# Value loads of five transfers a pair in place of seven, in a chunked-attention and Fourier-mixing kernel

## The chip, the cores and the metric

The kernel runs on one core of one Trainium2 chip. A core has five engines that each run a queue of their own in order: TensorE (PE in the profile, with its weight loads as PEld), VectorE (DVE), ScalarE (ACT), GpSimd (POOL) and SyncE (SP). Transfers between device memory and on-chip memory are issued by SP, ACT and POOL and carried by 16 DMA engines. The metric is the device time of one execution in microseconds (us), the median over the runs of a kernel.

## What is computed

The first half is attention in chunks with memory keys. There are 4 batches, 8 heads, 768 positions and a head size of 64. Each chunk of 32 queries sees 8 memory keys, up to 16 keys to its left, its own 32 and up to 8 to its right. The second half mixes the result with a two-dimensional Fourier transform (its real part), adds it, normalises each row and runs a two-layer network with 2048 hidden units. The part that the change touches is this:

```python
for c in range(nc):
    c_start = c * chunk
    c_end = c_start + chunk
    l_start = max(0, c_start - left_ctx)
    r_end = min(S, c_end + right_ctx)
    k_full = np.concatenate([mem_k, k[:, :, l_start:r_end]], axis=2)
    v_full = np.concatenate([mem_v, v[:, :, l_start:r_end]], axis=2)
    scores = scale * np.matmul(q[:, :, c_start:c_end], k_full.transpose(0, 1, 3, 2))
    a = np.exp(scores - np.max(scores, axis=-1, keepdims=True))
    a = a / (np.sum(a, axis=-1, keepdims=True) + 1e-09)
    out[:, :, c_start:c_end] = np.matmul(a, v_full)
```

## The kernel before, in words

**Tiles.** The work goes by pairs of heads, 16 in all (n = 0 to 15, four for each batch); hh is the head within a pair. Two chunks share a tile of 64 queries, so a head has NT = 12 tiles. The keys of a tile lie on partitions: 0 to 7 the memory keys, 8 to 23 the left context, 24 to 87 the tile's own 64 keys, 88 to 95 the right context, which makes KEYS = 96. What one of the two chunks may not see is masked in the exponential by a bias per partition, `mbias`, one column for each half of the queries.

**A pair's steps.** `e_load_qk` (L383) loads queries and keys from POOL's queue. `e_turn_q` and `e_turn_k` transpose them on PE (L415, into PSUM tiles trq and trk). `e_qT` (L433) copies the queries out on ACT; `e_kT` (L458; L453 for the last batch) copies the keys out with their overlap of left and right context, on DVE for n = 0 to 2, on ACT for n = 3 to 11 and on DVE again for the last batch. `e_scores` (L471) or `a_scores` (L494) multiplies, `e_exp` (L481) or `a_exp` (L506) takes the exponential, `e_values` (L523) multiplies the exponentials with the values in 48 small matmuls a pair (tiles xa and xo), and `e_norm` (L533, L534) divides by the sum, which column 64 of the value tile supplies through a column of ones. Each of the four value tiles `va` holds one pair in fp32, so a pair's values can be loaded once the pair that used its tile before it (n - 4) has been multiplied.

**The value loads.** `e_load_v` issues seven transfers a pair: the own keys of tile 0 for both heads (L399), and then for each head the run of 80 keys (left context and own keys) for tiles 1 to 11 (L392), the right context of 8 keys for tiles 0 to 10 (L392), and the 8 memory values for all tiles (L405). Every descriptor moves one row of 64 fp32 values, 256 bytes. All go through SP's queue, except that in the first batch the second head's long run is issued by ACT. `e_edges` zeroes what tile 0 lacks on its left and the last tile on its right, and `e_edge_ones` takes the ones from the sum column there; both run on POOL, for the first buffer partly on DVE.

**The order.** The kernel plans its order by costs, but the order on each engine is then fixed by lists at the end of the kernel, so the emission order is the same in both kernels. The scheduling layer gives each transfer that SP or ACT issues one of eight landing semaphores, in turn and in the order of the program. A transfer waits, besides for its buffer, until the one that had its semaphore before it, eight transfers of these two queues earlier, has landed. A queue is in order, so whatever stands behind such a transfer waits too. PE's queue also holds a fixed number of filler matmuls (L1040, L1048, tile dz), which do no work for the result.

**The rest.** After its pairs a batch is folded and multiplied with tables of sines (L729 and L768 for batch 0, L595 and later lines for the others), turned round and normalised, and then goes through the network (L908, L926, L975). The network's weights are loaded by POOL in eight transfers (L1269, L1274) during batch 1. For the batches after the first, rows travel out and back through device memory (L629, L633, L638).

Of the kernel before, what the change touches and what calls it, by code (L numbers as in the profile page):

```python
# [14 lines left out]
ALU = mybir.AluOpType  # L15

CHUNK = 32
LEFT = 16
RIGHT = 8
NMEM = 8  # L20
BIGM = 800.0
MEM0 = 0
OWN = MEM0 + NMEM + LEFT
KEYS = OWN + 2 * CHUNK + RIGHT


def rev_ap(src, last, count, outer=()):
# [5 lines left out]
def strided(src, off, dims):  # L33
    return bass.AP(tensor=src.tensor, offset=src.offset + off,
                   ap=[list(src.ap[0])] + [list(d) for d in dims])


class Plan:
# [14 lines left out]
    filling, fill, fine = None, None, None  # L53
# [155 lines left out]
def kernel(  # L209
# [11 lines left out]
    nc = tc.nc  # L221
    B, H, S, D = q.shape
    DM = out.shape[2]
    DFF = moe_w_ch1.shape[1]
    P = 128
# [3 lines left out]
    NT = S // 64  # L229
    RB = 8  # L230
    QP = S // RB
    KP = QP + 4
# [40 lines left out]
    NKT = 2  # L273
    KR, NKU = 16, 2
    kU = [spool.tile([P, KR + S + KR], BF16, name=f"kU{i}") for i in range(NKU)]
    kTb = [spool.tile([P, NT, P], BF16, name=f"kTb{i}") for i in range(NKT)]
# [36 lines left out]
    mbias = cpool.tile([P, 2], FP32)  # L313
# [24 lines left out]

    def e_masks():
        nc.gpsimd.memset(mbias, 0.0)  # L340
        nc.gpsimd.memset(mbias[64:96, 0:1], NEG)
        nc.gpsimd.affine_select(out=mbias[:, 1:2], in_=mbias[:, 1:2], compare_op=ALU.is_ge,
                                fill=NEG, base=-(OWN - LEFT + CHUNK), pattern=[[0, 1]],
                                channel_multiplier=1)
        nc.gpsimd.memset(mbias[MEM0:MEM0 + NMEM, 1:2], 0.0)
# [5 lines left out]
    def e_edges(i):  # L351
        v1, eng = va[i], nc.vector if i < 1 else nc.gpsimd
        eng.memset(v1[:, :, :, D:D + 1], 1.0)  # L353
        eng.memset(v1[0:32, :, 0, 0:D], 0.0)
        eng.memset(v1[64:96, :, NT - 1, 0:D], 0.0)

    def e_edge_ones(i):
        v1 = va[i]
        lo, hi = v1[0:32, :, 0, D:D + 1], v1[64:96, :, NT - 1, D:D + 1]
        nc.gpsimd.affine_select(out=lo, in_=lo, compare_op=ALU.is_ge, fill=0.0, base=-OWN,  # L360
                                pattern=[[0, 2], [0, 1]], channel_multiplier=1)
        nc.gpsimd.affine_select(out=hi, in_=hi, compare_op=ALU.is_ge, fill=0.0,
                                base=OWN + 63 - 64, pattern=[[0, 2], [0, 1]],
                                channel_multiplier=-1)
        nc.gpsimd.memset(v1[MEM0:MEM0 + NMEM, :, 0, D:D + 1], 1.0)

    def e_mkf():
# [18 lines left out]
    def e_load_v(n, half=None):  # L386
        b, pr = seq[n]
        v1 = va[n % NV]

        def run(p0, count, t0, nt, key, hh, by):  # L390
            vb = v[b, 2 * pr + hh]
            by.dma_start(v1[p0:p0 + count, hh, t0:t0 + nt, 0:D],  # L392
                              bass.AP(tensor=vb.tensor, offset=vb.offset + key * D,
                                      ap=[[D, count], [64 * D, nt], [1, D]]))

        if half == 1:
            run(OWN - LEFT, LEFT + 64, 1, NT - 1, 64 - LEFT, 1, nc.scalar)
            return
        nc.sync.dma_start(v1[OWN:OWN + 64, :, 0, 0:D],  # L399
                          v[b, 2 * pr:2 * pr + 2, 0:64].rearrange("h p d -> p h d"))  # L400
        for hh in range(2):
            if half is None or hh == 0:
                run(OWN - LEFT, LEFT + 64, 1, NT - 1, 64 - LEFT, hh, nc.sync)
            run(OWN + 64, RIGHT, 0, NT - 1, 64, hh, nc.sync)
            nc.sync.dma_start(v1[MEM0:MEM0 + NMEM, hh, :, 0:D],  # L405
                              mem_v[b, 2 * pr + hh].unsqueeze(1).to_broadcast([NMEM, NT, D]))

# [41 lines left out]

    def e_kT(n, eng=None):  # L450
        if n >= TURNED * HP:
            win = LEFT + 64 + RIGHT
            nc.vector.tensor_copy(  # L453
                strided(kTb[n % NKT], MEM0 + NMEM, [[P, NT], [1, win]]),
                strided(kU[n % NKU], KR - LEFT, [[64, NT], [1, win]]))
            return
        trk = tr_of.pop((n, 1))
        (eng or nc.scalar.copy)(  # L458
            strided(kTb[n % NKT], MEM0 + NMEM, [[P, NT], [RB, 11], [1, RB]]),
            strided(trk, 0, [[64 // RB, NT], [1, 11], [KP, RB]]))  # L460
        if n < 2 or n in JOINED:
            let_go(trk)

# [47 lines left out]
    def e_values(n, g):  # L511
        e1 = e1_of.pop((n, g))
        if g == 1:
            xa = bank("mlp" if n < HP else pick_of["v", n]["tag"], [P, 3, 2, 66], FP32, "xo")
        else:
            xa = aps.tile([P, 3, 2, 66], FP32, tag="xa", bufs=1, name="xa")
        xa_of[n, g] = xa
        for st in range(3):
            for hh in range(2):
                v1 = va[n % NV]  # L520
                for half in range(2):
                    t6 = 2 * st + half
                    nc.tensor.matmul(xa[64 * half:64 * half + 64, st, hh, 0:65],  # L523
                                     e1[0:KEYS, hh, t6, :], v1[0:KEYS, hh, 6 * g + t6, 0:65],
                                     start=True, stop=True)

    def e_norm(n, g):
# [1170 lines left out]
```

## Time and profile before

| What | Value |
|---|---|
| time, median of 3 runs | 272.72 us (272.63 to 278.22) |
| the profiled execution, its own time | 271.1 us |
| its span, first to last instruction | 269.4 us |
| PE busy, share of the span | 260.8 us, 97% |
| DVE, ACT and POOL busy | 202.7, 162.8 and 89.6 us |
| packets moved, bytes | 116118, 40.00 MB |
| of these under 512 bytes | 104560 |
| granted TensorE clock | 1.0 |

A busy share is an average over stages with different limits. The chain of waits follows the end of the program back, step by step, to what released each instruction. In a timeline row the numbers are the start and the length in us, then engine, line, operation and tiles, and in brackets how long the engine stood idle before it and what ended that. An engine name with a q behind it (SPq, ACTq) is that engine's queue issuing a transfer; the length then holds the time that the issue waited as well. In a row of a group the numbers behind the bar are busy us, mean ns of one instruction, and idle us before them. In a table by stretches each engine's busy us are followed by its number of instructions, and the last three numbers are the granted clock, the mean share of the DMA engines in use and GB/s.

### The profile page before, as it was taken

The page shows a single profiled execution, that of the slowest core. Times are in us where ns is not written, and L with a number is a line of the kernel's source. Part 1 is how long each engine was busy: PE and PEld are TensorE (multiplying, and loading weights), DVE is VectorE, ACT ScalarE, POOL GpSimd, SP SyncE. Part 2 cuts the span into 40 slices and gives each one's busy share as a digit, 9 for nine tenths or more (in the row PEclk, how much of TensorE's full clock was granted, in tenths as well). Part 3 has the DMA queues.
Part 4 walks back from the last instruction along what each step waited for, and adds up shares of the span by engine and source line. Part 5 has one row for each costly group of instructions (what it writes and reads, how often), then busy time and mean ns, then how long its engine had stood idle before and what let it go on. Part 6 is the DMA issues. An engine that isn't in the chain of part 4 may idle for free.

```text
span 269.4 us, 8363 instructions
## 1 busy us (share of the span) xinstructions
PE 260.8 (97%) x3469; PEld 215.8 (80%) x3469; DVE 202.7 (75%) x456; ACT 162.8 (60%) x318; POOL 89.6 (33%) x159
## 2 busy tenths in 40 slices
PE   6999899999999999999899999999999999999995
PEld 6556597888964778857798888888988988888884
DVE  6867488863379779999999989999887855354444
ACT  6757868899866279766742974726627171715150
POOL 7985463045120091564480550006006231000000
PEclk9999999999999999999999999999999999999999
DMA  6999999979998999989999974681913233334263
GB/s 102 206 180 191 211 195 200 213 126 195 197 241 169 130 218 175 126 222 206 197 218 161 159 169 88 165 130 19 238 20 82 61 77 80 89 61 108 56 166 92
DMA packets 116118, 40.00 MB, mean 148 GB/s; under 512 B 104560, under 2 KB 111472, under 8 KB 116080
## 3 DMA queue, kind: packets, MB, share of 16 engines
q1 hardware_dynamic: 90304, 22.64, 46.5%
q0 software_dynamic: 21472, 15.21, 34.8%
q10 hardware_dynamic: 4304, 1.62, 3.0%
q8 instruction: 27, 0.44, 0.7%
q14 instruction: 11, 0.09, 0.1%
HBM read 37.36 MB, written 13.37 MB: 188 GB/s over the span
## 4 chain that ended last, share of the span: by engine, by line
PE 73%; DVE 11%; DMA 8%; POOL 4%; issue 1%; SPq 1%; ACT 0%; POOLq 0%
PE ph L908 27%; PE pc L975 21%; PE pc L926 5%; PE ps L595 5%; DMA va<-in_v_dram 5%; DMA va<-in_mem_v_dram 3%; PE xa L523 3%; PE xo L523 3%; PE ps L729 2%; PE pm L768 2%; DVE st L843 1%; DVE xsb L534 1%; PE pm L789 1%; DVE xsb L817 1%; PE sc L494 1%
## 5 line engine op out<-in xcount | busy, mean ns | idle before, releaser
L908 PE MATMUL ph<-unT,w_sb 128*128 128x256 f16 x768 | 88.9, 273 | 0.2 <-DVE xsb L980 0.2
L917 ACT ACTIVATE hT<-ph 128x512 f16<-128x512 f32 x96 | 55.2, 600 | 51.6 <-PE pc L975 37.5
L908 PEld LDWEIGHTS <-w_sb 128*128 128x128 f16 x768 | 74.2, 98 | 9.7 <-issue 0.5
L975 PEld LDWEIGHTS <-hT 128*128 128x128 f16 x360 | 34.6, 98 | 4.5 <-DVE hT L963 0.2
L975 PE MATMUL pc<-w_sb,hT 128*128 128x256 f16 x288 | 36.6, 273 | 0.0
L980 DVE TENSOR_TENSOR xsb<-pc,xsb 128x256 f32<-128x256 f32 x64 | 26.1, 419 | 13.7 <-PE pc L975 12.8
L831 POOL TENSOR_TENSOR xsb<-mix,xr 128x512 f32<-128x512 f32 x9 | 12.3, 1384 | 42.3 <-ACT mix L825 24.4
L506 ACT ACTIVATE e<-sc,mbias 96x192 f32<-96x192 f32 (+1 forms) x48 | 19.0, 470 | 5.0 <-PE sc L494 5.0
L926 PE MATMUL pc<-w_sb,hT 128*128 128x512 f16 x96 | 21.7, 379 | 0.0
L481 ACT ACTIVATE e<-sc,mbias 96x384 f32<-96x384 f32 x32 | 17.0, 573 | 6.8 <-PE sc L471 6.8
L963 DVE TENSOR_TENSOR S<-hT 128x768 f16<-128x768 f16 (+1 forms) x18 | 7.6, 421 | 17.2 <-ACT hT L917 16.9
L857 ACT ACTIVATE un<-xsb,rs 128x512 f16<-128x512 f32 x18 | 14.4, 821 | 5.3 <-POOL rs L872 5.3
L975 PE MATMUL pc<-w_t,S 128*128 128x256 f16 x144 | 17.4, 273 | 0.0
L926 PEld LDWEIGHTS <-hT 128*128 128x128 f16 x96 | 9.1, 98 | 10.1
L843 DVE BATCH_NORM_STATS2 st<-xsb 128x6 f32<-128x512 f32 x24 | 16.3, 681 | 0.8 <-POOL xsb L831 0.6
L523 PE MATMUL xa<-va,e 96*64 96x65 f32 x384 | 14.9, 226 | 1.3 <-DMA va<-in_mem_v_dram 1.3
L523 PEld LDWEIGHTS xa<-va,e 96*64 96x64 f32 x384 | 12.6, 137 | 3.7 <-issue 2.9
L975 PEld LDWEIGHTS <-S 128*128 128x128 f16 x144 | 14.0, 98 | 1.6
L523 PE MATMUL xo<-va,e 96*64 96x65 f32 x384 | 14.1, 223 | 0.0
L1040 PE MATMUL idle<-dz 128*128 128x512 bf16 x46 | 12.9, 387 | 1.0 <-DVE va L353 1.0
L433 ACT COPY qT<-trq 128x768 bf16<-128x768 bf16 x12 | 9.6, 796 | 6.6 <-PE trq L415 6.4
L523 PEld LDWEIGHTS xo<-va,e 96*64 96x64 f32 x384 | 12.6, 138 | 0.4 <-ACT e L481 0.2
(192 smaller groups left out, 489.1 us busy)
## 6 DMA issues: line engine op xcount, KB each, us to landing
va<-in_v_dram SPq DMA_DIRECT2D x28, 220.0 KB
w_sb<-in_moe_w_ch_dram POOLq DMA_DIRECT2D x8, 512.0 KB, 9.0
out_dram<-xsb SPq DMA_DIRECT2D x12, 256.0 KB
qs<-in_q_dram POOLq DMA_DIRECT2D x12, 192.0 KB, 6.7
ks<-in_k_dram POOLq DMA_DIRECT2D x12, 192.0 KB, 6.6
x_rows<-xsb POOLq DMA_DIRECT2D x3, 768.0 KB, 5.1
xr<-x_back POOLq DMA_DIRECT2D x3, 768.0 KB, 5.7
out_rows<-xsb SPq DMA_DIRECT2D x9, 256.0 KB
```

Of the source, the lines that this page charges most:

```text
L481: nc.scalar.activation(e1[0:KEYS, :, :, ts(half, 32)], sc[0:KEYS, :, 0:6, ts(half, 32)], AFT.Exp, bias=mbias[0:KEYS, half:half + 1], scale ...
L506: nc.scalar.activation(to, src, AFT.Exp, bias=mbias[0:KEYS, half:half + 1], scale=1.0 / math.sqrt(D))
L523: nc.tensor.matmul(xa[64 * half:64 * half + 64, st, hh, 0:65], e1[0:KEYS, hh, t6, :], v1[0:KEYS, hh, 6 * g + t6, 0:65], start=True, stop=True)
L595: nc.tensor.matmul(out_[:, sp, :], part[:, ab, sp * 3 + st, c0:c1], tab[:, sp, st, :], start=(st == 0 and i == 0), stop=(st == 2 and i == 1))
L843: nc.vector.bn_stats(st6, xs[b][:, kt, :])
L857: nc.scalar.activation(un, xs[b][:, kt, :], AFT.Identity, bias=rs[:, 1:2], scale=rs[:, 0:1])
L908: nc.tensor.matmul(ph[:, k, :], w1_sb[:, dt, ts(HH * k + i, P)], unT_of[b, j][:, dt, :], start=(dt == 0), stop=(dt == NDT - 1))
L917: nc.scalar.activation(hT_of[b, j][:, :, i, :], ph, AFT.Relu, bias=0.0, scale=1.0 if (b, j) in FAST else -1.0)
L926: nc.tensor.matmul(pc_of[b, j, r], hT_of[b, j][:, k, i, ts(r, P)], w2_sb[:, HH * k + i, :], start=(i + k == 0), stop=(i + k == HH))
L975: nc.tensor.matmul(pc_of[key], a[:, i, :], w[:, i, :], start=(i == 0 and new), stop=(i == HH - 1), skip_group_check=not new)
L980: nc.vector.tensor_tensor(u, pc, u, ALU.add)
L1040: nc.tensor.matmul(fill_of[0], dz, strided(dz, 0, [[0, 4], [1, P]]), start=True, stop=True)
```

## The change

The value run of a tile gets 8 keys more than any chunk sees: AFTER = 16 keys follow the tile's own 64, and KEYS becomes 104. With that, one run of 96 keys for tiles 1 to 11 takes the place of the run of 80 and of the right context's own transfer, and tile 0's transfer takes 80 keys. A pair's loads are then five: tile 0 for both heads, and a run and the memory values for each head. The 8 extra keys are masked for both halves by `mbias`. The run of the last tile would read past the head's end, where the next head's rows lie; the values matmul of the last tile therefore takes only its first LAST = 88 partitions, and the very last head of the input, behind which nothing lies, has its last tile in a transfer of its own. The zeroing on the right and its part in the ones go away. The copies of the keys take 96 columns a tile in place of 88, and the exponentials 104 partitions in place of 96.

```diff
-KEYS = OWN + 2 * CHUNK + RIGHT
+AFTER = 2 * RIGHT
+LAST = OWN + 2 * CHUNK
+KEYS = LAST + AFTER
...
         nc.gpsimd.memset(mbias, 0.0)
-        nc.gpsimd.memset(mbias[64:96, 0:1], NEG)
+        nc.gpsimd.memset(mbias[64:P, 0:1], NEG)
+        nc.gpsimd.memset(mbias[96:P, 1:2], NEG)
...
         eng.memset(v1[0:32, :, 0, 0:D], 0.0)
-        eng.memset(v1[64:96, :, NT - 1, 0:D], 0.0)
...
-        lo, hi = v1[0:32, :, 0, D:D + 1], v1[64:96, :, NT - 1, D:D + 1]
+        lo = v1[0:32, :, 0, D:D + 1]
...
-        nc.gpsimd.affine_select(out=hi, in_=hi, compare_op=ALU.is_ge, fill=0.0,
-                                base=OWN + 63 - 64, pattern=[[0, 2], [0, 1]],
-                                channel_multiplier=-1)
...
+        def rows(hh, by):
+            whole = (b, 2 * pr + hh) != (B - 1, H - 1)
+            run(OWN - LEFT, KEYS - OWN + LEFT, 1, NT - 2 + whole, 64 - LEFT, hh, by)
+            if not whole:
+                run(OWN - LEFT, LEFT + 64, NT - 1, 1, S - 64 - LEFT, hh, by)
+
         if half == 1:
-            run(OWN - LEFT, LEFT + 64, 1, NT - 1, 64 - LEFT, 1, nc.scalar)
+            rows(1, nc.scalar)
             return
-        nc.sync.dma_start(v1[OWN:OWN + 64, :, 0, 0:D],
-                          v[b, 2 * pr:2 * pr + 2, 0:64].rearrange("h p d -> p h d"))
+        nc.sync.dma_start(v1[OWN:KEYS, :, 0, 0:D],
+                          v[b, 2 * pr:2 * pr + 2, 0:64 + AFTER].rearrange("h p d -> p h d"))
         for hh in range(2):
             if half is None or hh == 0:
-                run(OWN - LEFT, LEFT + 64, 1, NT - 1, 64 - LEFT, hh, nc.sync)
-            run(OWN + 64, RIGHT, 0, NT - 1, 64, hh, nc.sync)
+                rows(hh, nc.sync)
             nc.sync.dma_start(v1[MEM0:MEM0 + NMEM, hh, :, 0:D],
                               mem_v[b, 2 * pr + hh].unsqueeze(1).to_broadcast([NMEM, NT, D]))
...
-            win = LEFT + 64 + RIGHT
+            win = LEFT + 64 + AFTER
...
-            strided(kTb[n % NKT], MEM0 + NMEM, [[P, NT], [RB, 11], [1, RB]]),
-            strided(trk, 0, [[64 // RB, NT], [1, 11], [KP, RB]]))
+            strided(kTb[n % NKT], MEM0 + NMEM, [[P, NT], [RB, 12], [1, RB]]),
+            strided(trk, 0, [[64 // RB, NT], [1, 12], [KP, RB]]))
...
                     t6 = 2 * st + half
+                    rows = LAST if 6 * g + t6 == NT - 1 else KEYS
                     nc.tensor.matmul(xa[64 * half:64 * half + 64, st, hh, 0:65],
-                                     e1[0:KEYS, hh, t6, :], v1[0:KEYS, hh, 6 * g + t6, 0:65],
+                                     e1[0:rows, hh, t6, :], v1[0:rows, hh, 6 * g + t6, 0:65],
                                      start=True, stop=True)
```

The order of the instructions on every engine is otherwise unchanged. The landing semaphores are handed out over five transfers a pair, so other transfers share one: in the built program ACT's transfer for n = 3 waits for the landing of n = 1's first run in place of n = 1's tile 0.

## The prediction, made before the changed kernel was run

> **What bounds the kernel now.** I read the page's first part, then the chain of waits in order of time, then a table of the stretches that this chain divides.
>
> ```profile
> span 269.4 us, 8363 instructions
> PE 260.8 (97%) x3469; PEld 215.8 (80%) x3469; DVE 202.7 (75%) x456; ACT 162.8 (60%) x318; POOL 89.6 (33%) x159
> ```
> ```profile
> 8.62 7.09 DMA va<-in_v_dram
> 15.73 0.59 SPq L399
> ...
> 17.01 5.83 DMA va<-in_v_dram
> 22.85 0.27 SPq L392
> 23.16 9.32 DMA va<-in_mem_v_dram
> 32.62 0.80 PE xa L523 x20
> ```
> ```profile
> 32.60:41.10 8.50, 8.48 (x134) 7.97 (x135) 5.75 (x13) 6.16 (x13) 5.50 (x14) 1.00 1.15 197
> 45.80:98.60 52.80, 52.80 (x845) 40.25 (x847) 36.11 (x75) 38.28 (x68) 14.62 (x24) 1.00 1.05 183
> 98.60:130.00 31.40, 30.68 (x450) 24.06 (x450) 30.87 (x65) 23.97 (x57) 15.39 (x21) 1.00 1.28 191
> 180.00:266.00 86.00, 86.00 (x812) 76.96 (x810) 55.05 (x130) 38.51 (x75) 13.64 (x20) 1.00 0.37 85
> ```
>
> The chain runs through the value loads up to 32.6 us, and through PE after that. It looks as if 24 us of loading were to be won, but a chain shows only the last arrival. PE was busy all that time too, with fillers, transposes and attention whose number and order are fixed. What the loads cost is PE's idle time in front of the matmul that waited:
>
> ```profile
> 30.95 0.34 PE L523 MATMUL xa<-va,e 96*64 96x65 f32 x4
> ...
> 32.62 0.80 PE L523 MATMUL xa<-va,e 96*64 96x65 f32 x20 [1.33 <-DMA va<-in_mem_v_dram]
> ```
>
> In the view of waits this is the only wait of PE for a value load, 1.33 us, for the last memory values of n = 3. From 32.6 us to the end PE is dense (the table's first number behind the stretch is PE's busy time), so what is gained here stays gained, and nothing else that the loads do can shorten the time. In the stretch from 98.6 to 130 us DVE is dense as well.
>
> **Part 1, the loads start earlier: minus 1.33 us.** The last value transfers of n = 3 were late because their issues were held in SP's queue, and then because they met the weights:
>
> ```profile
> 15.73 0.59 SPq L399 DMA_DIRECT2D va<-in_v_dram  x1
> ...
> 23.16 0.31 SPq L405 DMA_DIRECT2D va<-in_mem_v_dram  x1
> ```
> ```profile
> 22.94 1.12 POOL L1269 DMA_DIRECT2D w_sb<-in_moe_w_ch_dram  x2
> ```
>
> The first transfer of n = 2 went out at 15.73 us, when n = 1's run, eight transfers ahead, had landed (the chain: 8.62 + 7.09 = 15.71). The last of n = 3 went out at 23.16, just behind two weight loads of 512 KB each, and took 9.32 us where the right context of n = 2, issued at 17.01 and as small, took 5.83. With five transfers a pair, eight places reach back more than a pair and a half. Followed through the changed order, tile 0 and run of n = 2 wait only for n = 0's memory values and go out near 10 us; tile 0 and run of n = 3 wait for n = 1's memory values, issued right behind its run, near 17 us; the last memory values of n = 3 wait for an ACT transfer of n = 1 and for n = 2's tile 0, and I put them at 19 us. With those 5.83 us they land near 25 us, and even with 9.32 us near 28.5, ahead of the 30.95 at which PE asks. So the whole stall goes. What is late next at that place is PE itself. The bounds of this part are 0 and -1.33 us.
>
> **Part 2, a new wait in ACT's queue: plus 0.2 us.** The changed hand-out of semaphores moves the wait that stood in SP's queue at 15.73 into ACT's. ACT's transfer for n = 3 now waits for n = 1's run, and behind it stands the copy of n = 1's queries:
>
> ```profile
> 13.35 0.32 ACTq L392 DMA_DIRECT2D va<-in_v_dram  x1
> 13.76 0.57 ACT L481 ACTIVATE e<-sc,mbias 96x384 f32<-96x384 f32 x1
> 14.22 0.79 ACT L433 COPY qT<-trq 128x768 bf16<-128x768 bf16 x1
> 16.21 1.04 ACT L481 ACTIVATE e<-sc,mbias 96x384 f32<-96x384 f32 x2 [1.20 <-PE sc L471]
> ```
> ```profile
> 13.54 0.51 PE L415 MATMUL trq<-ident_b,qs 96*64 96x96 bf16 x16
> ...
> 17.27 0.54 PE L415 MATMUL trk<-turn_b,ks 100*64 100x100 bf16 x16
> ...
> 18.28 0.35 PE L471 MATMUL sc<-qT,kTb 64*128 64x64 bf16 x12
> ```
>
> The copy would start at L, the landing of n = 1's run, and not at 14.22. It frees the PSUM tile that PE's trk at 17.27 writes, and the exponentials behind it (1.04 us) free the scores' tile for PE at 18.28. A release took 14.22 - (13.54 + 0.51) = 0.17 us. So PE is held when L + 0.79 + 0.17 passes 17.27, or L + 0.79 + 1.04 + 0.17 passes 18.28: both from L = 16.3 us on, and from there each us of L costs PE one, because PE's fillers don't shrink. L was 15.71. For the changed L:
>
> ```profile
> DMA packets 3153, 0.93 MB, mean 199 GB/s; under 512 B 2977, under 2 KB 3152, under 8 KB 3152
> ...
> q10 hardware_dynamic: 1618, 0.41, 57.4%
> q1 hardware_dynamic: 1339, 0.33, 50.9%
> ```
> ```profile
> 8.72 1.33 POOL L362 TENSOR_SCALAR_AFFINE_SELECT va<-va 32x2 f32<-32x2 f32 x1
> ...
> 11.14 0.65 POOL L383 DMA_DIRECT2D qs<-in_q_dram  x1
> ```
>
> The first fence is the DMA view from 11 to 15.7 us: SP (q1) and ACT (q10) moved 2957 packets in 4.7 us, 629 a us. Tile 0 and run of n = 1 grow from 128 + 880 to 160 + 1056 packets, 208 more, or 0.33 us, and twice that when ACT's longer runs take turns with them. POOL loses a memset and a select for each buffer, among them the select of 1.33 us, so its query load at 11.14 starts up to about 1.8 us earlier and gets ahead of the run: 192 KB at 199 GB/s, up to 0.97 us. Against that, SP's issue for n = 1 no longer waits for a memset that ends at 8.1, some 0.4 us. L lies between 15.3 (none of the delays) and 15.71 + 0.66 + 0.97 = 17.3; the middle is 16.3, just where the cost begins. The cost is 0 to 1.0 us, and I take 0.2, as half of the cases lie below the threshold. If the cover is gone altogether, this part eats most of part 1.
>
> The Trainium skill speaks against the change here: its page "DMA: Bandwidth & Descriptors", section "Bandwidth", says that small descriptors pay a fixed overhead for each packet, so fewer transfers of more packets cost more. The page of the profile agrees: 90304 packets on SP's queue (q1) took 46.5% of 16 engines' span, 22 ns each, so 208 more cost 0.29 us of all engines for a pair, less than the 0.33 us above, which goes by the same count.
>
> ```profile
> q1 hardware_dynamic: 90304, 22.64, 46.5%
> ```
>
> The skill's same page, section "Why a DMA increments its semaphore by 16 and not by 1", says that a transfer of SP or ACT over 8 partitions uses only the lowest 8 of the 16 engines; no row here shows which engines. By that rule the fullest engines would go from 8 + 110 + 46 = 164 to 10 + 132 + 24 = 166 packets a pair, an estimate of 1% and not 9%, and rival C below would fall away; the sum would stay, since it prices the run, which uses all 16.
>
> **Part 3, wider copies and more rows: plus 0.2 us.**
>
> ```profile
> L415 PE MATMUL trk<-turn_b,ks 100*64 100x100 bf16 x192 | 6.4, 209 | 0.0
> L415 PE MATMUL trq<-ident_b,qs 96*64 96x96 bf16 x192 | 6.2, 207 | 1.1 <-DVE ident_b L1015 1.1
> ...
> L458 DVE COPY kTb<-trk 128x1056 bf16<-128x1056 bf16 x3 | 3.8, 1253 | 1.7 <-PE trk L415 1.7
> ```
> ```profile
> L453 DVE COPY kTb<-kU x4: 402/426/428, 117.4 to 157.3; 128x1056 bf16<-128x1056 bf16 x4
> ```
> ```profile
> L523 PE MATMUL xa<-va,e 96*64 96x65 f32 x384 | 14.9, 226 | 1.3 <-DMA va<-in_mem_v_dram 1.3
> ...
> L523 PE MATMUL xo<-va,e 96*64 96x65 f32 x384 | 14.1, 223 | 0.0
> ```
>
> The copies grow from 1056 to 1152 columns, by 9%: 0.11 us for each of the three early ones on DVE, about the same for the nine on ACT, 0.04 for the four of the last batch. The early ones stand ahead of PE's scores, with fillers as cover; without that cover they would cost 0.34 us, and I take 0.1. ACT's nine lie beside dense PE: nothing, or 1.0 us uncovered. The four lie in DVE's dense stretch, 0.15 us, of which I take 0.1. The value matmuls go from 96 to 104 rows. The nearest rows are transposes with 100 and with 96 rows, 209 and 207 ns with 100 and 96 columns, so 4 more rows show nothing of their own: 0. As an upper bound in proportion to the rows, the value matmuls' busy time of 14.9 + 14.1 = 29.0 us would grow by 8.3%, 2.4 us. The removed memsets and selects on POOL, and one memset more there, touch only part 2.
>
> **The sum.** -1.33 + 0.2 + 0.2 = -0.9 us. The profiled execution took 271.1 us with a span of 269.4, and would take 270.2. The median of the runs shown, 272.72, lies 1.6 us above the profiled one, so on that scale I forecast 271.8 us.
>
> **The rivals.**
>
> A: the wait only moves. L becomes 17.3 us or later, PE stands at trk for 1.0 us or more, and with the 0.2 of part 3 the stall's 1.33 us are used up: 272.6 us. For it speaks that SP, ACT and POOL compete in those microseconds; against it that SP issues earlier.
>
> B, the other side: more rows cost PE time. It decides as soon as a value matmul takes over 3% longer, since 3% of 29.0 us is 0.9. In full proportion: 272.72 - 0.9 + 2.4 = 274.2 us. The transposes speak against it.
>
> C: volume. Each pair moves 2464 packets and not 2256. Before, the last weights went out at 64.80 us; 11.7 us later, the longest landing of a weight load, they were there, at 76.5; PE's matmuls that read this layer begin at 77.80:
>
> ```profile
> 64.80 1.59 POOL L1274 DMA_DIRECT2D w_sb<-in_moe_w_ch_dram  x2
> ```
> ```profile
> DMA to landing us min/median/max: 7.3/9.0/11.7
> ```
> ```profile
> 77.80 4.32 PE pc L926 x20
> ```
>
> If all the 9% fell on that landing, it would be 1.1 us later and just meet PE's 77.80. With twice that PE would lose 1 us: 272.8 us. Only the last quarter of these weights is so late and it is read last, which speaks against it, as do the earlier starts of the value loads.
>
> D: no effect. The last values of n = 3 meet the weights anyway and land when PE asks or later, with the stall as before: 272.9 us with part 3.
>
> **How the numbers follow.** The forecast has a chance of 0.58, A 0.18, B 0.08, C 0.06, D 0.06, and 0.04 is left for what I don't see. The likeliest case by itself reaches from full gain without costs, 272.72 - 1.33 = 271.4, to 272.4. The median of another set of runs can differ by some tenths; I take 270.8 as the low end, which also covers part of the 1.6 us between the two scales, and 273.4 as the high end, which takes in A, C, D and half of B. About 2% is what a measurement of this kernel can tell from no change, 5.5 us here. No case comes near it in either direction, so within 2% has 0.94, and slower, where unseen waits can add up on a dense PE, 0.04; faster 0.02.
>
> **What would show it.** Part 1: no idle time before L523's matmuls near 31 us, n = 3's last L405 issue before 21 us. Part 2: the ACTq row at 13.35 moves to the landing of n = 1's run, and L433's copy with it; an idle time of PE before trk near 17 us is its price. Part 3: L458 at about 1.37 us on DVE, L523 still at 222 ns. The prediction is wrong if PE's idle time grows anywhere after 33 us, if L523 gets longer, or if the stall at 32.6 us stays.

## The result, and the profile after

The changed kernel took 272.92 us (median of 22 executions, 271.31 to 276.08), the kernel before 271.88 us (22, 269.56 to 278.24). Over the executions that can be compared the ratio is 1.0095, with an interval of 1.007 to 1.012: about 2.6 us of 270 slower, and not 0.9 us faster. Medians are over all executions, while ratios leave out those that were disturbed, so the two need not agree. Of the 19 executions of the changed kernel in the ratio, ten have a mean granted clock of 0.999 or 1.0, with spans of 269.6 to 271.4 us, and nine have 0.988 or 0.994, with spans of 271.0 to 273.3 us.

The profiled execution, one of the nine, took 273.75 us, with a span of 272.0 us against 269.4. The page's first part, and then the chain of waits from 7.5 to 21 us (start, duration, what):

```profile
span 272.0 us, 8306 instructions
PE 263.5 (97%) x3469; PEld 217.7 (80%) x3469; DVE 202.9 (75%) x455; ACT 163.9 (60%) x318; POOL 87.5 (32%) x153
```
```profile
8.12 10.07 DMA va<-in_v_dram
...
18.22 0.32 ACTq L391
...
18.58 0.81 ACT qT L437
...
19.43 0.56 PE trk L419 x16
```

n = 1's run was issued 0.5 us earlier than before and took 10.07 us instead of 7.09, so L, its landing, is 18.20 and not 15.71 us. ACT's transfer for n = 3 goes out at 18.22 (before: 13.35), the query copy behind it at 18.58 (14.22), and trk starts at 19.43 instead of 17.27. PE's timeline gives the idle time, and the table of stretches what came behind it; the column that ends the engines' busy times is the granted clock:

```profile
19.43 0.56 PE L419 MATMUL trk<-turn_b,ks 100*64 100x100 bf16 x16 [1.99 <-ACT qT L437]
```
```profile
17.30:20.00 2.70, 0.71 (x18) 0.59 (x18) 0.00 (x0) 1.42 (x3) 1.48 (x2) 0.97 1.36 183
20.00:23.00 3.00, 3.00 (x39) 1.91 (x40) 2.08 (x4) 1.39 (x3) 0.00 (x0) 0.50 1.31 198
23.00:24.00 1.00, 1.00 (x15) 0.34 (x13) 0.69 (x2) 0.00 (x0) 0.00 (x0) 0.88 1.23 185
24.00:32.60 8.60, 8.33 (x189) 5.67 (x181) 5.83 (x12) 6.67 (x12) 4.11 (x7) 1.00 1.00 161
```

PE stood for 1.99 us, and then worked at half its clock for some 3.4 us: from 20 to 23 us it ran 39 matmuls. By the clock column, 0.03 of 2.7 us, 0.50 of 3 us and 0.12 of 1 us weren't granted, together 1.7 us that are lost while PE counts as busy. So in this execution the one wait cost 1.99 + 1.7 = 3.7 us, and the second part shows in no list of waits, only in the clock. The ten executions with a mean clock of 0.999 or more can have no such stretch, since it takes 0.006 off the mean (1.7 of 272 us).

What the prediction wanted to be gone is gone. These are SP's last issues for n = 3 (before: 22.85 and 23.16), and the groups of L528 (before L523), of the early copies on DVE and of the fillers (busy us, mean ns | idle before):

```profile
20.62 0.64 SPq L409 DMA_DIRECT2D va<-in_mem_v_dram  x2
```
```profile
L528 PE MATMUL xa<-va,e 104*64 104x65 f32 x384 | 14.7, 226 | 0.0
L528 PE MATMUL xo<-va,e 104*64 104x65 f32 x320 | 14.6, 229 | 0.0
L1045 PE MATMUL idle<-dz 128*128 128x512 bf16 x46 | 13.5, 401 | 1.0 <-DVE va L356 1.0
L462 DVE COPY kTb<-trk 128x1152 bf16<-128x1152 bf16 x3 | 4.1, 1354 | 3.7 <-PE trk L419 3.7
```

The last memory values of n = 3 landed at 27.94 us, and xa has no idle time. A value matmul of 104 rows into xa takes the 226 ns that one of 96 took before, and one into xo takes 229 instead of 223. The 229 hold the 24 that ran at half the clock; in late_gate1 below, where the clock never falls, xa and xo have 226 and 223 ns again:

```profile
L528 PE MATMUL xa<-va,e 104*64 104x65 f32 x384 | 14.9, 226 | 0.2 <-DMA va<-in_mem_v_dram 0.2
L528 PE MATMUL xo<-va,e 104*64 104x65 f32 x320 | 14.0, 223 | 0.0
```

The fillers' mean of 401 ns (before: 387) is the low clock again.

### The profile page after: what moved, and what is told of

The parts are those of the page before. It is cut to its first block, busy times and chain, and to the rows that moved or that the text cites. A ratio compares the mean times of both kernels' runs of the same rounds, so it can differ in the third digit from the quotient of the medians.

```text
span 272.0 us, 8306 instructions
## 1 busy us (share of the span) xinstructions
PE 263.5 (97%) x3469; PEld 217.7 (80%) x3469; DVE 202.9 (75%) x455; ACT 163.9 (60%) x318; POOL 87.5 (32%) x153
## 4 chain that ended last, share of the span: by engine, by line
PE 79%; DVE 9%; DMA 4%; POOL 4%; ACT 2%; issue 1%; ACTq 0%; SPq 0%; POOLq 0%
PE ph L913 27%; PE pc L980 21%; PE pc L931 5%; PE ps L600 5%; PE xa L528 4%; PE xo L528 4%; DMA va<-in_v_dram 4%; PE ps L734 3%; PE idle L1045 2%; PE pm L773 2%; PE sc L475 2%; DVE st L848 1%; PE trk L419 1%; PE pm L794 1%; PE trq L419 1%
## 5 line engine op out<-in xcount | busy, mean ns | idle before, releaser
L510 ACT ACTIVATE e<-sc,mbias 104x192 f32<-104x192 f32 (+1 forms) x48 | 19.2, 483 | 4.9 <-PE sc L498 4.9
L931 PE MATMUL pc<-w_sb,hT 128*128 128x512 f16 x96 | 21.7, 379 | 0.0
L485 ACT ACTIVATE e<-sc,mbias 104x384 f32<-104x384 f32 x32 | 17.2, 582 | 6.6 <-PE sc L475 6.6
L848 DVE BATCH_NORM_STATS2 st<-xsb 128x6 f32<-128x512 f32 x24 | 16.3, 681 | 0.8 <-POOL xsb L836 0.6
L528 PE MATMUL xo<-va,e 104*64 104x65 f32 (+1 forms) x384 | 14.7, 228 | 0.0
L528 PE MATMUL xa<-va,e 104*64 104x65 f32 x384 | 14.7, 226 | 0.0
L1045 PE MATMUL idle<-dz 128*128 128x512 bf16 x46 | 13.5, 401 | 1.0 <-DVE va L356 1.0
L528 PEld LDWEIGHTS xa<-va,e 104*64 104x64 f32 x384 | 12.5, 137 | 2.3 <-issue 1.5
L528 PEld LDWEIGHTS xo<-va,e 104*64 104x64 f32 (+1 forms) x384 | 13.2, 143 | 0.5 <-ACT e L485 0.2
```

Of the source, the lines that this page charges most:

```text
L485: nc.scalar.activation(e1[0:KEYS, :, :, ts(half, 32)], sc[0:KEYS, :, 0:6, ts(half, 32)], AFT.Exp, bias=mbias[0:KEYS, half:half + 1], scale ...
L510: nc.scalar.activation(to, src, AFT.Exp, bias=mbias[0:KEYS, half:half + 1], scale=1.0 / math.sqrt(D))
L848: nc.vector.bn_stats(st6, xs[b][:, kt, :])
L931: nc.tensor.matmul(pc_of[b, j, r], hT_of[b, j][:, k, i, ts(r, P)], w2_sb[:, HH * k + i, :], start=(i + k == 0), stop=(i + k == HH))
L1045: nc.tensor.matmul(fill_of[0], dz, strided(dz, 0, [[0, 4], [1, P]]), start=True, stop=True)
```

## The experiments

The theory, called W, is that the moved wait is the loss: ACT's queue stands until L, PE behind it, and the clock falls. The rivals are the rows, the volume and the order of the loads. Unless a number is said to be a ratio or a median, it is from the profiled execution. For each ratio the kernel before was run on the same chip.

**late_act: ACT's transfer behind the exponentials.** One entry of ACT's list is moved:

```
-... 47, 73, 59, 51, 63, 67, ...
+... 47, 59, 51, 63, 73, 67, ...
```

> The changed kernel with one move in ACT's written order: ACT's value transfer for n = 3 is issued behind the exponentials of n = 1's first scores instead of ahead of the copy of n = 1's queries. Nothing else moves. Theory W (the wait in ACT's queue holds the query copy until n = 1's run has landed at 18.2 us; PE stands 1.99 us before trk, and the clock that then falls to 0.50 for some 3.5 us costs another 1.7 to 2): PE's idle time before trk at 17.3 us falls under 0.3 us, the granted clock stays 1.0 from 17 to 24 us, and with the stall at 32.6 us gone as in the changed kernel the span is 268.1 to 268.9 us, 3.1 to 3.9 under the changed kernel's 272.0 and about 0.7 under the kernel before: a ratio of 0.996 to 0.998. Rival R (the loss is the longer value matmuls and copies, spread over the kernel): the span stays at 271 us or more, ratio 1.006 or more. Rival V (the loss is the DMA volume, which delays the weights): no change of the ratio either, with idle time of PE behind 57 us. If n = 3's values become late by the later issue (it would be some 19 to 20 us), a stall at 31 to 33 us comes back and the span is 269.5 to 270.

Measured: span 271.6 us, ratio 1.0112 (1.0058 to 1.0166). The wait before trk is gone and the clock is 1.0 throughout, yet the time isn't. The planner fills what it takes for idle time of PE, and for the new order it put in 55 fillers instead of 46. PE's timeline has the nine:

```profile
25.66 2.12 PE L1045 MATMUL idle<-dz 128*128 128x512 bf16 x9
```

They cost 2.1 us in front of a dense PE, so this run tells nothing about W by its time. It was done again as late_kept.

**fill_in: nine fillers into the gap.**

```
 def e_turn_k(n):
+    for _ in range(9 if n == 2 else 0):
+        e_fill()
```

> The changed kernel with nine more filler matmuls of PE (they compute nothing that is used) put directly ahead of the transposes trk of n = 2, where PE now stands idle for 1.99 us. The wait in ACT's queue stays as it is. Theory W2 (of the 2.5 to 3.5 us lost, about half is the wait itself and the other half is the clock that falls to 0.50 because PE stood idle): the fillers take the place of the idle time, trk starts at 19.4 us as in the changed kernel or up to 0.3 later, the granted clock stays 1.0 from 20 to 24 us, and the span is 270.2 to 270.7 us, 1.3 to 1.8 under the changed kernel: a ratio to the kernel before of 1.003 to 1.005. Rival (the clock falls for another reason, such as the load on the other engines in those microseconds): the clock still shows 0.50 there and the span is 272 us or more. Rival N (the low clock costs nothing, because PE catches up in waits behind it): clock 1.0, but the span stays at 271.8 to 272.3 us.

Measured: ratio 1.0098 (1.0051 to 1.0145), a miss. In the profiled execution, the longest of the twelve (span 274.1 us), trk starts at 19.21 us without idle time and the clock is 1.0 up to 27 us. Then comes another wait, which the view of PE ascribes to no engine:

```profile
27.30 0.27 PE L530 MATMUL xo<-va,e 88*64 88x65 f32 x1 [2.49 <-issue]
```

After it the clock falls to 0.50 too. Five of its twelve executions had spans of 269.9 to 270.9 us, in or within 0.3 us of the 270.2 to 270.7 of W2, and the others were longer. That a busy PE keeps its clock agrees with W2; how much it saves stays open here.

**pool_kept: POOL's removed work put back.**

```
         eng.memset(v1[0:32, :, 0, 0:D], 0.0)
+        eng.memset(kU[0][64:96, 0:2 * D], 0.0)
...
+        hi = kU[0][64:96, 0:2]
+        nc.gpsimd.affine_select(out=hi, in_=hi, ...)
```

> The changed kernel with POOL's removed work put back: the memset and the select of each buffer for the masked keys behind the last tile run again, on other memory whose content is overwritten before use, so POOL's query load of n = 2 goes out near 11.1 us, as before the change, and not at 8.8. Theory Q (n = 1's run lands at 18.2 us and not near 17 because the earlier query load got ahead of its packets): the run lands at 16.8 to 17.4 us, PE's idle time before trk is 0.5 to 1.1 us, the clock falls for a shorter time or not at all, and the span is 269.6 to 271.0 us, ratio 1.000 to 1.006. Rival T (the run lands late because the transfers themselves became longer, and ACT's with them): it lands at 17.9 us or later, the span stays at 271.6 to 272.3 us, ratio 1.008 to 1.011.

Measured: span 270.4 us, ratio 1.0058 (1.0002 to 1.0114). POOL's query load goes out at 11.07 us (changed kernel: 8.78). The chain, and PE's row:

```profile
8.43 8.45 DMA va<-in_v_dram
```
```profile
18.11 0.54 PE L423 MATMUL trk<-turn_b,ks 100*64 100x100 bf16 x16 [0.76 <-ACT qT L441]
```

L is 16.88 us, the wait is 0.76 us, and the clock stays at 1.0. That is what theory Q expected. But one trace doesn't show Q: in late_gate2, fill_in, late_act and late_kept, with the same loads ahead of it as in the changed kernel, L was 17.03, 17.32, 17.53 and 17.62 us. So it varies by more than a microsecond from one execution to another, the 18.20 of the changed kernel's profile is the top of it, and 16.88 lies only 0.15 us below the rest.

**rows_only: the wider runs without the fewer transfers.**

```
-            rows(1, nc.scalar)
+            run(OWN - LEFT, LEFT + 64, 1, NT - 1, 64 - LEFT, 1, nc.scalar)
...
+            run(OWN + 64, AFTER, 0, NT - 1, 64, hh, nc.sync)
```

> The kernel before with the wider runs alone: the value buffers hold eight more keys, the value matmuls read 104 rows, the copies are 1152 columns wide, POOL's memsets and selects are as in the changed kernel, but each pair still has seven value transfers, the right context being a transfer of its own with 16 keys. So the volume grows as in the changed kernel, and the semaphores are handed out as in the kernel before. Theory W (only the moved wait costs): no idle time of PE before trk at 17 us, the clock stays 1.0, the stall before xa at 32.6 us stays (1.0 to 2.0 us), and the span is 269.4 to 270.2 us, ratio 1.000 to 1.003. Rival R (rows cost PE time in proportion): L523's mean goes from 226 to 240 ns or more and the span to 271.8 us, ratio 1.009. Rival V (volume): span 270.4 us or more with idle time of PE behind the weights at 57 to 81 us.

Measured: span 275.7 us, ratio 1.0235 (1.0176 to 1.0294). All three theories missed. There is no wait before trk; L523's mean is 231 ns, so the rows are not it; and PE has no idle time from 57 to 81 us. The stall that the kernel before had at 32.6 us grew. The chain, POOL's row of the weights and PE's rows:

```profile
17.60 6.78 DMA va<-in_v_dram
...
24.39 0.28 SPq L404
...
25.66 10.89 DMA va<-in_mem_v_dram
```
```profile
23.15 1.12 POOL L1269 DMA_DIRECT2D w_sb<-in_moe_w_ch_dram  x2
```
```profile
33.66 0.34 PE L523 MATMUL xa<-va,e 104*64 104x65 f32 x4 [2.36 <-DMA va<-in_mem_v_dram]
36.68 1.10 PE L523 MATMUL xa<-va,e 104*64 104x65 f32 x15 [2.69 <-DMA va<-in_mem_v_dram]
```

SP's queue stood until n = 2's run had landed at 24.38 us, so n = 3's memory values were issued at 24.39 and 25.66, behind the two weight loads issued from 23.15 us on, and the last took 10.89 us. Together 5.05 us of idle time, and a clock of 0.73 from 36 to 45.8 us. So with seven transfers the added keys don't fit ahead of the weights. It needn't be the volume alone: this kernel also has the changed kernel's shorter work on POOL, and so its earlier query load of n = 2 (8.79 us; the kernel before: 11.14), which no run here separates from it. The five transfers, with the same keys and the same work on POOL, have no such stall, and bring the new wait.

**late_kept: only ACT's transfer moved.** The plan of the changed kernel is kept, and task 73 is emitted later:

```
+        placed = plan.settled(lists)
+        late = plan.tasks[73]
+        placed.remove(late)
+        placed.insert(placed.index(plan.tasks[63]) + 1, late)
```

> The changed kernel with ACT's value transfer for n = 3 behind the exponentials of n = 1's first scores, as in late_act, but with every other instruction left where the changed kernel has it: PE's 46 fillers and the order of its transposes and scores too, which the planner had changed in late_act (55 fillers). Theory W (the wait in ACT's queue, and the clock that falls behind it, are the loss): PE's idle time before trk near 17.3 us is under 0.3 us, the clock is 1.0 to 45 us, and the span is 268.2 to 269.3 us, 2.7 to 3.8 under the changed kernel's 272.0. The kernel before, whose compared runs have spans of 267.8 to 271.4, is then met or beaten: ratio 0.995 to 1.001. Rival P (late_act was no better because the loads themselves come late, not because of the fillers): span 271 us or more, with idle time of PE in front of xa or xo between 23 and 36 us. A smaller part may come from value loads of n = 5 or 6 that are late near 61 us: 0.3 to 0.9 us.

Measured: span 270.2 us. Of its six executions one more was that short (269.4), and four took 273.8 to 275.7 us; of the kernel before, nine of twelve took 267.8 to 269.4 us beside it. With two there is no interval. PE's rows:

```profile
17.27 0.54 PE L419 MATMUL trk<-turn_b,ks 100*64 100x100 bf16 x16
```
```profile
60.70 0.80 PE L528 MATMUL xa<-va,e 104*64 104x65 f32 x20 [1.08 <-DMA va<-in_mem_v_dram]
```

trk starts at 17.27 us, as before the change, and the clock is 1.0 to 45 us and beyond. This is W's prediction for the wait; in P's place, 23 to 36 us, there are only 0.55 us in front of sc at 24.21. But only 1.8 of the 3.7 us come out at the end: 1.08 us are given back at 60.70, where PE, now earlier, meets values that the changed kernel's PE found landed.

**runs_88: no masked keys.**

```
-AFTER = 2 * RIGHT
+AFTER = RIGHT
...
-    strided(kTb[n % NKT], MEM0 + NMEM, [[P, NT], [RB, 12], [1, RB]]),
+    strided(kTb[n % NKT], MEM0 + NMEM, [[P, NT], [RB, 11], [1, RB]]),
```

> The changed kernel with runs of 88 keys, without the eight masked keys: five transfers a pair as in the changed kernel, but the packets of the kernel before, value matmuls of 96 rows, and copies of 1056 columns. The wait of ACT's transfer for n = 1's run is as in the changed kernel. Theory V (the run lands at 17.3 to 18.2 us because each pair moves 9% more packets): it lands at 16.2 to 17.2 us, PE's idle time before trk is 0 to 0.9 us, the clock stays 1.0, span 268.2 to 269.8 us, ratio 0.995 to 1.003. Theory Q (it lands late because POOL's query load of n = 2 goes ahead of it, and the 9% do little): it lands at 17.2 us or later, idle time 1.0 us or more, span 270.3 us or more, ratio 1.004 or more. Rival R (rows and wider copies cost the time): the idle time stays and the span falls by the 0.3 us of the copies or by more than 1 us without less idle time.

Measured: span 276.3 us, ratio 1.0295 (1.0244 to 1.0347). V missed. The numbers of Q are met (the run lands at 19.82 us, PE stands for 2.22 us), but what follows points at another cause. The chain, and two stretches (last column: GB/s):

```profile
8.19 11.63 DMA va<-in_v_dram
...
21.03 0.54 PE trk L419 x16
```
```profile
13.00:20.00 7.00, 5.81 (x96) 3.36 (x95) 4.17 (x6) 2.56 (x5) 6.33 (x10) 1.00 0.91 141
20.00:30.00 10.00, 8.97 (x167) 5.78 (x166) 5.77 (x12) 5.68 (x11) 1.53 (x4) 0.83 0.85 148
```

The run of 88 keys took 11.63 us although it is smaller. The queues moved 141 GB/s from 13 to 20 us; the changed kernel moved 191. In the trace a run of 96 or 80 keys raises its landing semaphore 16 times, and one of 88 keys 12 times. The Trainium skill's page "DMA: Bandwidth & Descriptors", section "Why a DMA increments its semaphore by 16 and not by 1", says that such a transfer uses the largest number of engines up to 16 that divides its count, and that the issuing side adds the rest at once. By that rule 88 keys use 11 engines and 96 use 16; the 12 events, 11 landings and one jump, agree. By that rule the eight masked keys are what makes the run fill all engines. So this run doesn't test V or Q: it changes the number of engines together with the volume.

**gate_late: the kernel before with POOL's gate opened by n = 3's last values.**

```
-                nc.gpsimd.tensor_copy(gate[64:65], va[n % NV][64:65, 1, NT - 1, 0:1])
+                nc.gpsimd.tensor_copy(gate[0:1], va[n % NV][0:1, 1, NT - 1, 0:1])
```

> The kernel before with one edit in POOL's gate, the copy that holds the query and key loads of n = 4 and the weights back: it reads a memory row of n = 3's values, whose transfer is the last of n = 3, and no longer a row of ACT's transfer. Seven transfers, rows and order are as before. Theory G (the kernel before stalls at 32.6 us because two weight loads are issued just ahead of n = 3's last values, and the changed kernel lost that stall because its gate opened late): the query and key loads of n = 4 go out at 24 us or later and the weights behind them, n = 3's last values land by 29 us, no idle time of PE at 31 to 33 us, span 267.8 to 268.8 us, ratio 0.992 to 0.998, and none or few of its runs above 272 us. Rival S (SP's queue alone makes them late, by the seven transfers): the last values still land after 31 us and the stall stays at 1 us or more, span 269.2 us or more, ratio 1.000. Rival L (the late gate only moves the wait): idle time of PE for n = 4's queries or keys near 36 to 45 us, span 269 to 271 us.

Measured: one of six executions has a span of 269.6 us, the other five 275.9 to 278.0, where G expected few so long. The profile is of one of the five, span 275.9. In it the stall at 32.6 us is gone and the wait stands elsewhere:

```profile
59.51 0.34 PE L523 MATMUL xa<-va,e 96*64 96x65 f32 x4 [1.20 <-DMA va<-in_mem_v_dram]
64.22 1.03 PE L523 MATMUL xa<-va,e 96*64 96x65 f32 x14 [4.38 <-DMA va<-in_mem_v_dram]
```

The weights went out at 28.74 instead of 22.94 us, and later value loads met them. G holds for the stall, and not for the time. L is right that the wait moves, but to value loads at 60 us and not to queries or keys at 36 to 45. The size can't be taken from this execution.

**late_88: late_kept and runs_88 together.**

> late_kept and runs_88 together: the changed kernel with 88 keys a run and with ACT's transfer for n = 3 behind the exponentials. If the wait in ACT's queue is the whole loss, this is no better than late_kept by more than the 0.2 us of the copies: span 268.0 to 269.0 us, ratio 0.994 to 1.000. If the volume has a cost of its own (later value loads, waits of PE between 23 and 62 us), it is 0.5 to 1.5 us under late_kept.

Measured: span 280.2 us, ratio 1.0412 (1.0382 to 1.0442). Both cases of the expectation missed. It adds nothing to the two: the runs of 88 keys again make the values late, here with 5.28 and 2.57 us in front of xa at 65.69 and 68.74 us.

**late_gate1 and late_gate2: late_kept with an earlier gate.**

```
-                nc.gpsimd.tensor_copy(gate[64:65], va[n % NV][64:65, 1, NT - 1, 0:1])
+                nc.gpsimd.tensor_copy(gate[64:65], va[1][64:65, 1, NT - 1, 0:1])    # late_gate1
+                nc.gpsimd.tensor_copy(gate[0:1], va[2][0:1, 0, NT - 1, 0:1])        # late_gate2
```

> late_kept with one more edit: POOL's gate, which holds back the query and key loads of n = 4 and the weights, reads ACT's value transfer of n = 1 (landed at 19.7 us in late_kept) and no longer that of n = 3 (26.9 us). So these loads go out near 20 us as in the kernel before, and the first weights near 23 and not 30 us. Theory B (late_kept gained 3.7 us at 24 us and gave 1.7 back, 1.08 of it at 60.7 us, since its weights went out 7 us later and n = 5's values shared the DMA engines with them): the wait at 60.7 us falls under 0.3 us; n = 3's values, issued by 20.1 us ahead of the weights, land by 31 us, so the stall there stays under 0.5 us; span 268.2 to 269.3 us, ratio 0.995 to 1.001, and fewer runs above 273 us than late_kept had (4 of 6). Rival M (the DMA engines are simply full, so an earlier gate moves the wait back to n = 3): idle time of PE of 1 us or more at 30 to 34 us, span 269.5 us or more.

> As late_gate1, but the gate reads the first memory transfer of n = 2, which landed at 21.2 us in late_kept. The loads behind it go out 1.5 us later than in late_gate1 and 5.7 us earlier than in late_kept. Theory B: between the two; n = 3's values have more room, the wait at 60.7 us is under 0.6 us, span 268.2 to 269.5 us. Rival M: waits of PE at both places that add up to 1 us or more, span 269.5 us or more.

Measured: late_gate1 span 269.1 us, ratio 1.0091 (1.0037 to 1.0144); late_gate2 span 271.7 us, ratio 1.0038 (0.999 to 1.0085). PE's rows of the one and of the other:

```profile
59.58 0.80 PE L528 MATMUL xa<-va,e 104*64 104x65 f32 x20 [0.22 <-DMA va<-in_mem_v_dram]
```
```profile
25.50 0.26 PE L475 MATMUL sc<-qT,kTb 64*128 64x64 bf16 x5 [1.64 <-issue]
```

In late_gate1's profile the wait near 60 us falls from 1.08 to 0.22 us and none comes back at 31 us: that agrees with B about the cause of what late_kept gave back. But its ratio missed what B expected: the ten executions that it uses spread from 269.1 to 273.0 us. late_gate2's profile met a wait of 1.64 us inside the scores, with a clock drop behind it. Neither is faster than the kernel before.

**before_again: a second trace of the kernel before.** No edit.

> The kernel before once more, for a second trace. The spans of its compared runs lie between 267.8 and 271.4 us, and the prediction was worked out from one of 269.4 that had a stall of 1.33 us at 32.6 us. If that stall is a matter of when the last values of n = 3 land, a run of 267.8 to 268.6 us has no idle time there, and one above 270 us has more of it; everything else in PE's order is the same to 0.2 us.

Measured: span 268.5 us. Its first line, and PE's rows:

```profile
span 268.5 us, 8363 instructions
```
```profile
31.03 0.92 PE L523 MATMUL xa<-va,e 96*64 96x65 f32 x24
...
59.05 0.80 PE L523 MATMUL xa<-va,e 96*64 96x65 f32 x20 [0.41 <-DMA va<-in_mem_v_dram]
```

The stall of 1.33 us that the prediction was built on isn't there. Of the 37 executions of the kernel before that can be compared in the four sets of experiments, 26 were shorter than the profiled 269.4 us.

**wait_only: the kernel before with the wait alone.**

```
         if half == 1:
+            if n == 3:
+                nc.scalar.copy(held[64:65], va[1][64:65, 1, NT - 1, 0:1])
```

> The kernel before with the wait alone: ahead of ACT's value transfer for n = 3, ACT copies one element of n = 1's values that ACT's own transfer brought (it landed at 17.95 us in the profile of before), so ACT's queue stands until then and the copy of n = 1's queries with it. Seven transfers, volume, rows and POOL's work are as before. Theory W (the wait in ACT's queue with the clock behind it is the loss of the changed kernel): the copy of the queries ends near 19.1 us, PE stands 1.7 to 2.1 us before trk, the clock falls to 0.50 for some 3.3 us (1.6 us more), and the span is 270.8 to 272.0 us, where the trace of before without a stall had 268.5: ratio 1.008 to 1.013. Rival (the changed kernel's loss needs its volume too, and PE wins the wait back in later waits for values): span 270 us or less, ratio 1.005 or less. If the landing is under 17 us by chance, the wait is under 1 us and the clock stays 1.0.

Measured: span 271.8 us, the shortest of six, which reach up to 278.5. The ten of the kernel before beside them took 268.1, 268.3 and then 273.2 to 275.8 us, so there are too few short ones for an interval. ACT's rows, PE's, and the stretches:

```profile
17.75 0.19 ACT L398 COPY held<-va 1x1 f32<-1x1 f32 x1 [3.42 <-DMA va<-in_v_dram]
...
18.12 0.80 ACT L435 COPY qT<-trq 128x768 bf16<-128x768 bf16 x1 [0.19 <-issue]
```
```profile
18.98 0.55 PE L417 MATMUL trk<-turn_b,ks 100*64 100x100 bf16 x16 [1.64 <-ACT qT L435]
```
```profile
20.00:23.00 3.00, 3.00 (x40) 2.04 (x39) 2.23 (x5) 1.04 (x2) 0.00 (x0) 0.51 0.99 176
23.00:24.00 1.00, 1.00 (x24) 0.58 (x24) 0.00 (x0) 0.16 (x1) 0.18 (x1) 0.77 0.08 19
```

With the old rows, volume and POOL work, the wait alone brings the span to that of the changed kernel (272.0): 268.5 + 1.64 of waiting + 1.7 by the clock = 271.8. Together with late_kept, where the wait goes by moving one transfer, this shows what the wait and the low clock behind it cost in a profiled execution. It doesn't show that they are all that the changed kernel loses on the mean; that is taken up below.

## Why the prediction was wrong, point by point

**Part 1, the loads start earlier (-1.33): right in mechanism, too large.** The issues came 1 to 2 us later than forecast (n = 2 from 11.22 us on, n = 3 from 18.56, the last at 20.94, landed at 27.94), still in time, and rows_only shows what the five transfers are worth with these keys. But 1.33 us was the stall of one execution; before_again has none there. Most of the gain that the sum counted wasn't there to be had.

**Part 2, the new wait in ACT's queue (+0.2): the step that failed.** The place, the wait and the queue behind it were named rightly, and the threshold of 16.3 us fits: 18.20 - 16.3 = 1.9 us, measured 1.99. The term that was mis-sized is L: put between 15.3 and 17.3 us and taken as 16.3, with half of the cases free of cost, it was 18.20 in the profile, and 16.88 to 17.62 us in the five others named above. All six lie above the threshold. I had added the delays (0.66 us for the wider runs, 0.97 for the earlier query load, 0.4 off) as if each load only waited for the packets put ahead of it; but the run, the query load and ACT's two runs, issued from 8.12 to 10.05 us, were in flight together, and the run took 10.07 us. Single traces say that each delay alone is over a microsecond: L is 15.40 to 15.87 us in the four traces with the old runs and the late query load (before, before_again, gate_late, wait_only), 16.88 with the wider runs alone (pool_kept), and 16.95 with the earlier query load and the old run of 80 keys (rows_only). And the slope was wrong: it isn't one microsecond for each of L, since behind the idle times of 1.5 us and more the clock fell, for 1.7 us on top. Rival A, with a chance of 0.18, was the right case; its 272.6 us lacked the clock and counted the stall of 1.33 us as gained.

**Part 3, copies and rows (+0.2): right.** DVE's copies take 1354 ns (forecast 1.37 us), L528 226 to 229 ns. PE's busy time in late_gate1, where the clock never falls, is 262.3 us against 262.0 in before_again; the first trace of the kernel before has 260.8, so this comparison is good to about a microsecond only.

**Rival B (rows)** is refuted by those durations. **Rival C (volume)** was put at the last weights; rows_only has a cost, at the value loads of n = 3, if that is volume. **Rival D** didn't occur: the stall was gone.

In numbers: the changed kernel's 272.0 is 3.5 us above before_again's 268.5. The parts are 1.99 of waiting, 1.7 by the clock, 0.27 in front of sc at 27.29, an estimated 0.1 for the copies, less the 0.41 at 59.05, which PE no longer meets: 3.65.

That explains one execution of each kernel, and not the mean loss of 2.6 us. Ten executions of the changed kernel took 269.6 to 271.4 us without the low clock, where 26 of the 37 of the kernel before stay under 269.4. They may have the wait in a shorter form, as pool_kept has with 0.76 us and a clock of 1.0; no trace shows one of them. And late_gate1 and late_gate2, in whose profiles there is no wait before trk, have ratios of 1.0091 and 1.0038 where the changed kernel has 1.0095; their shortest spans are 269.1 and 269.2 us, against 267.8 of the kernel before beside them. So about a microsecond or more is lost in another way too. Their profiles show waits marked "issue" (0.54 us in late_gate1, 0.37 and 1.64 in late_gate2) and a late value load (0.22); no run isolates them, and this part of the cause stays open.

## What to carry to other kernels

When fewer transfers change how landing semaphores are handed out, list for each transfer which landing it now waits for, and what stands behind it in its engine's queue: a wait that was harmless on a queue that only loads is dear on an engine that also feeds PE. Take a second trace before a stall of one execution is counted as gain, and don't settle for the middle of a range when a cost begins inside it: here the landing of n = 1's run lay between 16.88 and 18.20 us in six traces, all beyond the threshold. Price PE's idle time with the clock that follows it, and look past the mended place: in late_kept about half of the 3.7 us didn't come out, 1.08 of it at the next late load.

## What the runs showed of the hardware that was not expected

- **A short wait halves the clock.** Idle times of 1.29, 1.33 and 1.40 us (late_88, before, runs_88) left the granted clock at 1.00; 1.51 (runs_88 at 65.33 us), 1.64, 1.99 and 2.22 us were followed by 0.50 for about 3.4 us. The Trainium skill's page "TensorE: Matmul & The Clock Gate", section "Part 1: The HAM clock gate (the "warmup" mystery)", says that the clock halves after at least one idle window of about 3.4 us. The length of the low stretch agrees with that window; the idle time that sufficed here was less than half of it. The clock record of the traces says more. Each low stretch inside the program lasts 3.41 us, or two or three times that where more waiting followed (6.83 in rows_only, 10.24 in late_88), and the two of runs_88, from 21.72 and 66.10 us, begin 13 times 3.41 us apart. In the six cases of a single such stretch (one each in the changed kernel, fill_in, late_gate2 and wait_only, two in runs_88) the idle time lay in the 3.41 us before the fall (in the changed kernel 17.44 to 19.43 us, the fall at 19.83). So it seems that the idle share of windows on a fixed grid decides, which is inferred from these few cases; whether a longer wait across the border of two windows goes free, no run shows.
- **PE may wait for its own code.** The waits marked "issue" in the middle of a group (0.27 to 2.49 us, near 24 to 27 us) follow a 16 KB packet of the instruction queue (q8): it ended at 25.68, 25.81, 22.61 and 23.59 us in the changed kernel, fill_in, late_kept and late_gate2, and PE went on at 27.29, 27.30, 24.21 and 25.50, 1.5 to 1.9 us later each time. In the two traces of the kernel before it ended at 21.2 and 21.7 us, and PE had no such wait. That the packet holds what PE waits for, and that it was late because of the value loads, is argued from the times; no run here isolates it.
- **A smaller transfer can be slower**: the run of 88 keys took 11.63 us and that of 96 keys 10.07. The traces show the times and the 12 and 16 events; that the count of engines is the reason follows from the rule cited at runs_88.
